# Attention in half-rows of TensorE: both heads' scores and both halves of a transposed block emitted in turn, middle rows as one full-row product

## Chip, core and metric

One core of one Trainium2 chip. The metric is device time in microseconds; the kernel before takes 741.76 us in the median of three runs.

## What is computed

Attention over 16 (batch, head) pairs with pooled queries, then two feed-forward blocks on its 1152 x 512 output:

```python
q_pool = q.reshape(B, H, S // 2, 2, D).mean(axis=3)       # B 2, H 8, S 1152, D 64
scores = scale * np.matmul(q_pool, k.transpose(0, 1, 3, 2))
scores = scores - np.max(scores, axis=-1, keepdims=True)
attn = np.exp(scores); attn = attn / (np.sum(attn, axis=-1, keepdims=True) + 1e-09)
x = np.matmul(attn, v)                                    # rows to 1152 tokens x 512
g = x @ w_gate; x = (g / (1 + np.exp(-g)) * (x @ w_val)) @ w_out      # d_ff 1536
h = x @ w_in; out = (np.maximum(h, 0) + alpha * np.minimum(h, 0)) @ w_out2   # d_ff 2048
```

## The kernel before

**Stages.** Heads are handled in eight pairs: head 0 of a pair lies on partitions 0 to 63, head 1 on 64 to 127. A pair has 576 pooled query rows per head, cut into nine units of 128 rows of scores: four units for each head, and one middle unit that holds the first 64 rows of both heads. After the eight pairs come the feed-forward blocks (contract, L791; out1, L851; out2, L880).

**A unit.** The scores of a unit stand against 1152 keys in three cuts of 448, 448 and 256 columns, each in one PSUM bank (four banks "s"). Queries and keys are split into a high and a low part in a rounded format ("fed"), and three products (high-high, low-high, high-low; TERMS) make one cut: L639, a matmul over one 64-row half of the array. The middle unit is not split: L633, plain fp32 from the raw q and k ("plain"), one 64 x 64 corner of the array for each head. DVE copies a cut out of PSUM with a running extreme (L643), ACT takes the exponential with a row sum (L645). Then the 128 x 1152 block is transposed on TensorE (L666): each of nine chunks as two transposes, rows 0 to 63 and rows 64 to 127, 64 columns out of each, collected five and four at a time in banks "t" (three of them). A bank is moved to SBUF by ACT (L679) or DVE (L673); a counter gives DVE a quarter of them. When a group of units is through (5/9, then 4/9 of a pair) the product with the values follows (L700): plain fp32, all 128 rows, 64 columns for each head, so the two heads run side by side; nine key chunks x two heads in a group. Row sums are inverted (L711 to L714), sent through DRAM and multiplied in by POOL.

**Order.** Nothing is emitted in loop order. Each operation is a task with an engine, a planned duration, a priority and buffers; Plan.run fills engine after engine in planned time and emits in that order. PE has three queues: PE (whole array) and PE0, PE1 (ROWS: the 64-row halves), the two halves planned independently, each task on its own planned end. On the chip all of them stand in one instruction stream. Going from half rows to whole rows has a planned price ("turnon"). While nothing fits early on, both halves idle, small matmuls on zeros (L361) are emitted. Weights of the feed-forward blocks are loaded from the first transpose of the last pair on ("begun") and split by ACT and DVE (L476 to L484).

## Time and profile before

| what | us |
|---|---|
| median of three runs (739.19 to 751.92) | 741.76 |
| profiled execution | 734.53 |
| its span, first to last instruction | 732.7 |
| PE busy, share of the span | 98% |
| DVE, ACT, POOL busy | 65%, 49%, 12% |
| mean granted TensorE clock | 0.959 |

The span is that of the profiled execution; the other 1.8 us lie around it. A matmul's duration in a row includes its passage through the array, and matmuls overlap: what a stream of them costs is read from the distance of starts. The granted clock is a share of 2.4 GHz; 0.50 is 1.2 GHz.

### The profile page before, as it was taken

How to read it: one execution, taken by the hardware profiler on the slowest of the kernel's cores; microseconds unless marked ns; L12 is line 12 of the kernel's file. 1: busy time of each engine (PE TensorE's matmuls, PEld its weight loads, DVE VectorE, ACT ScalarE, POOL GpSimd, SP SyncE). 2: the span in 40 equal slices, each digit the busy share in tenths (PEclk: the TensorE clock that was granted, in tenths of full speed). 3: DMA queues.
4: the chain of work that ended last, by engine and by line, in shares of the span. 5: the costliest groups of instructions: out<-in, count | busy, mean ns of one | idle time of the engine just before them, and what ended most of it. 6: DMA issues, size and time to landing. Idle time of an engine off the chain costs nothing.

```text
span 732.7 us, 12409 instructions
## 1 busy us (share of the span) xinstructions
PE 720.4 (98%) x4919; PEld 609.3 (83%) x4919; DVE 473.7 (65%) x976; ACT 355.4 (49%) x651; POOL 87.9 (12%) x83
## 2 busy tenths in 40 slices
PE   6999999999999999999999999999999999999998
PEld 4657676857676767899999999999999899898886
DVE  4455555757564657899987569557889729754332
ACT  3346566858574768545444343223067546342210
POOL 2222222333312101100000000002400000000000
PEclk7589979999997999999999999999999999999999
DMA  4213121311210202433435113310213401100002
GB/s 129 65 34 98 32 84 36 97 65 51 66 50 33 79 19 86 159 146 115 160 129 167 64 57 116 116 58 14 102 58 116 138 36 61 54 1 0 1 34 96
DMA packets 16650, 55.37 MB, mean 76 GB/s; under 512 B 2192, under 2 KB 2832, under 8 KB 16592
## 3 DMA queue, kind: packets, MB, share of 16 engines
q1 hardware_dynamic: 16512, 54.46, 21.9%
q8 instruction: 38, 0.62, 0.3%
q14 instruction: 20, 0.16, 0.1%
q10 hardware_dynamic: 80, 0.11, 0.1%
HBM read 52.17 MB, written 2.40 MB: 74 GB/s over the span
## 4 chain that ended last, share of the span: by engine, by line
PE 96%; DVE 1%; DMA 1%; ACT 1%; issue 0%; DVEq 0%
PE bank L791 33%; PE bank L880 14%; PE bank L639 12%; PE bank L700 10%; PE bank L851 10%; PE bank L666 10%; PE bank L633 6%; DMA plain<-in_kt 1%; PE bank L361 0%; DMA plain<-in_qt 0%; DVE magnitudes L480 0%; ACT weights L481 0%; PE bank L713 0%; ACT et L679 0%; DVE et L673 0%
## 5 line engine op out<-in xcount | busy, mean ns | idle before, releaser
L791 PE MATMUL bank<-xh,weights 128*128 128x384 f32 x960 | 253.6, 337 | 0.6 <-DVE weights L484 0.6
L791 PEld LDWEIGHTS bank<-xh,weights 128*128 128x128 f32 x960 | 174.4, 188 | 3.5 <-DVE weights L484 1.0
L791 PE MATMUL bank<-xl,weights 128*128 128x384 f32 x480 | 161.4, 336 | 0.0
L639 PE MATMUL bank<-fed 64*128 64x448 f32 (+1 forms) x576 | 130.0, 391 | 6.5 <-ACT fed L569 4.5
L666 PEld LDWEIGHTS bank<-ident,plain 64*128 64x128 f32 x1296 | 92.2, 145 | 39.3 <-issue 18.0
L643 DVE TENSOR_SCALAR_CACHE_REDUCE plain<-bank,stats 128x448 f32<-128x448 f32 (+1 forms) x144 | 82.5, 579 | 58.6 <-PE bank L639 42.7
L666 PE MATMUL bank<-ident,plain 64*128 64x64 f32 x1296 | 108.8, 238 | 0.8 <-DVE et L673 0.3
L679 ACT ACTIVATE et<-bank 128x320 f32<-128x320 f32 (+1 forms) x216 | 79.7, 423 | 56.8 <-PE bank L666 52.8
L639 PEld LDWEIGHTS bank<-fed 64*128 64x128 f32 x576 | 87.5, 206 | 16.7 <-issue 6.3
L645 ACT ACTIVATE plain<-plain,stats 128x1152 f32<-128x1152 f32 x72 | 90.8, 1267 | 11.5 <-DVE plain L643 10.7
L791 PEld LDWEIGHTS bank<-xl,weights 128*128 128x128 f32 x480 | 90.2, 188 | 1.2
L700 PE MATMUL bank<-et,plain 128*64 128x256 f32 (+1 forms) x576 | 79.9, 431 | 0.0
L880 PE MATMUL bank<-wr,fed 128*128 128x512 f32 (+1 forms) x279 | 70.4, 387 | 0.0
L700 PEld LDWEIGHTS bank<-et,plain 128*64 128x64 f32 x576 | 43.7, 145 | 30.4 <-issue 6.1
L643 DVE TENSOR_SCALAR_CACHE_REDUCE plain<-bank 128x448 f32<-128x448 f32 x72 | 44.7, 621 | 30.7 <-PE bank L639 29.2
L831 ACT ACTIVATE plain<-bank,signs 128x384 f32<-128x384 f32 x48 | 27.9, 582 | 70.3 <-PE bank L791 70.1
L880 PEld LDWEIGHTS bank<-wr,fed 128*128 128x128 f32 x279 | 51.1, 188 | 10.4
L832 DVE SCALAR_TENSOR_TENSOR plain<-bank,signs,plain 128x384 f32<-128x384 f32 x48 | 29.5, 615 | 36.2 <-ACT plain L831 36.2
L851 PE MATMUL bank<-fed,wr 128*128 128x384 f32 x264 | 52.2, 338 | 0.0
L673 DVE COPY et<-bank 128x256 f32<-128x256 f32 x72 | 30.4, 422 | 27.5 <-PE bank L666 21.7
L851 PEld LDWEIGHTS bank<-fed,wr 128*128 128x128 f32 x264 | 46.8, 188 | 0.0
L633 PE MATMUL bank<-plain 64*64 64x448 f32 (+1 forms) x96 | 44.9, 572 | 0.0
(75 smaller groups left out, 775.6 us busy)
## 6 DMA issues: line engine op xcount, KB each, us to landing
plain<-in_w_out SPq DMA_DIRECT2D x28, 512.0 KB
plain<-in_w_in SPq DMA_DIRECT2D x16, 512.0 KB
plain<-in_w_gate SPq DMA_DIRECT2D x12, 512.0 KB
plain<-in_w_val SPq DMA_DIRECT2D x12, 512.0 KB
plain<-in_vt SPq DMA_DIRECT2D x8, 576.0 KB
plain<-in_qt SPq DMA_DIRECT2D x7, 576.0 KB
plain<-in_kt SPq DMA_DIRECT2D x7, 576.0 KB
plain<-rowd SPq DMA_DIRECT2D x16, 144.0 KB
```

The source lines that it names most:

```text
L633: add(ROWS[h], 4 * w / 2400.0 + 0.0075, lambda s=s, rows=rows, js=js, w=w: nc.tensor.matmul(s.ap[rows, :w], x.qm.ap[rows], x.kn.ap[rows, j ...
L639: nc.tensor.matmul(s.ap[:, :w], x.qhl.ap[rows, a * SQ + c0:a * SQ + c0 + P], x.khl.ap[rows, b * S + js.start:b * S + js.stop], start=k == ...
L643: add(DVE, dve(w) + 0.056, lambda s=s, js=js, w=w, i=i: nc.vector.tensor_scalar(e.ap[:, js], s.ap[:, :w], 1.0, m(i - 1) if i else None, AL ...
L645: add(ACT, act(S, True, True), lambda: nc.scalar.activation(e.ap, e.ap, AF.Exp, bias=m(2), scale=-1.0, accum_out=x.sums.ap[:, n:n + 1]), p ...
L666: add(ROWS[h], HALFTURN, lambda t=t, c=c, ks=ks, rows=rows: nc.tensor.transpose(t.ap[:, c * D:c * D + D], e.ap[rows, ks:ks + P], ident[row ...
L673: go(dst, t.ap[:, :size * D].rearrange("p (c q) -> p c q", q=D))
L679: add(ACT, act(size * D), lambda move=move: move(lambda d, s: nc.scalar.activation(d, s, AF.Copy)), pr, [(t, 0)], [tok], [t, b])
L700: nc.tensor.matmul(acc.ap[rows, :n], x.vn.ap[:, h * SQ + kc * D:h * SQ + kc * D + D], ets[h][blk].ap[:, at:at + n], start=kc == 0, stop=kc ...
L791: nc.tensor.matmul(acc.ap[:, :TB], l[:, cs], r[:, c, ts], start=c == 0 and a == 0, stop=c == KC - 1 and a == 2)
L832: add(DVE, dve(TB) + 0.056, lambda: nc.vector.scalar_tensor_tensor(u.ap, a.ap[:, :TB], sign(), u.ap, ALU.mult, ALU.max), prio, [a], [u], [ ...
L851: nc.tensor.matmul(acc.ap[:, :TB], l[:, os_], r, start=n == 0 and m == 0, stop=n == len(g) - 1 and m == 2)
L880: nc.tensor.matmul(acc.ap[:, :width], l, r[:, cols], start=n == 0 and m == 0, stop=n == len(g) - 1 and m == 2)
```

## The change

The two half-row queues become one (HALF). A score task now emits the matmul of head 0 and of head 1 right after each other, so a unit is done for both heads at a time (five steps a pair: the middle one and four double ones). A transpose task holds a whole bank's worth, upper and lower half in turn. The middle unit becomes a whole-row product: the queries of both heads stand in two 64 x 64 corners of a 128 x 128 block whose rest is zero (corner), split into high and low like the others, three terms; POOL makes the corners with four copies of 64 x 64 per pair. Eviction of a transposed bank goes to whichever of ACT and DVE the planner finds (EITHER). The planner now prices a switch between half and whole rows in both directions; its priorities (KNOB) are others, among them vstep 0.321 for 0.007: the product with the values is planned key chunk by key chunk. The first pair's loads come in two pieces for both heads where there were pieces per head. The feed-forward code is not touched.

```diff
-ROWS = ("PE0", "PE1")
+HALF = "PEH"
+EITHER = "ACT or DVE"
...
+            full, half = self.pick(PE, now, hold[PE], port), self.pick(HALF, now, hold[PE], port)
+            if full and half:
+                if full[0] + (knobs["push"] if halves else -knobs["stay"]) <= half[0]:
+                    heapq.heappush(wait[HALF], half)
+                    half = None
                 else:
...
+            if full or half:
+                begin((full or half)[2], now, knobs["turnon"] if halves != bool(half) else 0.0)
...
+            elif now < 40.0 and not self.classes["acc"]["next"]:
+                self.idle()
...
+    corner = stat.tile([P, 2, 2 * P], F32R, name="corner")
+    nc.gpsimd.memset(corner.bitcast(F32), 0.0)
...
-        x.qcuts = [(0, 0, N0), (0, N0, SQ), (1, 0, SQ)] if first else [(None, 0, SQ)]
-        x.kcuts = [(0, *c) for c in CUTS] + [(1, 0, S)] if first else [(None, 0, S)]
+        x.qcuts = [(None, 0, N0), (None, N0, SQ)] if first else [(None, 0, SQ)]
+        x.kcuts = [(None, *c) for c in CUTS] if first else [(None, 0, S)]
...
-        add(POOL, gp(D), lambda: nc.gpsimd.tensor_scalar(x.qm.ap, x.qn.ap[:, :D], QSCALE, 1.0, ALU.mult, ALU.mult), K["first"] if first else s0, [(x.qn, i) for i, c in enumerate(x.qcuts) if c[1] == 0], [x.qm], [x.qn, x.qm])
+        for a in range(2):
+            for h in range(2):
+                r = rows(h)
+                add(POOL, gp(D), lambda a=a, h=h, r=r: nc.gpsimd.tensor_scalar(x.qm.ap[r, a * P + h * D:a * P + h * D + D], qpart(a, slice(0, D), r).bitcast(F32), 1.0, 1.0, ALU.mult, ALU.mult),
...
-    OF = [[0, 1, 5, 2, 6], [3, 7, 4, 8]]
-    OF0 = [[1, 2, 5, 0, 6], [3, 7, 4, 8]]
+    OF = [[0, 1, 2], [3, 4]]
+    OF0 = [[1, 0, 2], [3, 4]]
...
-            for h in range(2) if head == 2 else ():
-                rows = slice(h * D, h * D + D)
-                add(ROWS[h], 4 * w / 2400.0 + 0.0075, lambda s=s, rows=rows, js=js, w=w: nc.tensor.matmul(s.ap[rows, :w], x.qm.ap[rows], x.kn.ap[rows, js], start=True, stop=True),
...
-                add(ROWS[head], beside(w), go, pos + turn("qk", p, n), rd, [(s, head)], [s, x.qhl, x.khl])
...
+                    for k, (a, b) in enumerate(TERMS):
+                        nc.tensor.matmul(s.ap[:, :w], x.qm.ap[:, a * P:a * P + P], x.khl.ap[:, b * S + js.start:b * S + js.stop], start=k == 0, stop=k == 2)
+                add(PE, 3 * mm(w), go, at, [(x.qm, a, h) for a in range(2) for h in range(2)] + x.kread(js.start, js.stop), [(ss[0], 2)], [ss[0], x.qm, x.khl])
...
+                    for h in range(2):
+                        rows = slice(h * D, h * D + D)
+                        nc.tensor.matmul(ss[h].ap[:, :w], x.qhl.ap[rows, a * SQ + c0:a * SQ + c0 + P], x.khl.ap[rows, b * S + js.start:b * S + js.stop], start=k == 0, stop=k == 2)
+                add(HALF, beside(w), go, at, rd, [(s, 2) for s in ss], [*ss, x.qhl, x.khl])
...
-                    add(ROWS[h], HALFTURN, lambda t=t, c=c, ks=ks, rows=rows: nc.tensor.transpose(t.ap[:, c * D:c * D + D], e.ap[rows, ks:ks + P], ident[rows, rows]),
...
+                    for c in range(size):
+                        ks = (at + c) * P
+                        for h in range(2):
+                            rows = slice(h * D, h * D + D)
+                            nc.tensor.transpose(ts[h].ap[:, c * D:c * D + D], e.ap[rows, ks:ks + P], ident[rows, rows])
...
+                add(HALF, HALFTURN * size, go, pr + turn("t", p, n), [(e, 0)], [(t, 0) for t in ts] + mark, [*ts, e])
...
-                if moved[0] * K["evd"] % 36 >= K["evd"]:
...
+                    task = add(EITHER, 0.0, None, q, [(t, 0)], [tok], [t, b])
```

What it moves, by the order of instructions on PE. Half-way through a pair in the kernel before, the middle unit (L633, 64 x 64) and the transposes and scores around it:

```order
L639 MATMUL bank<-fed 128x256
L633 MATMUL bank<-plain 64x448
L639 MATMUL bank<-fed 128x256 x2
L666 MATMUL bank<-ident,plain 128x64 x4
L633 MATMUL bank<-plain 64x448
L666 MATMUL bank<-ident,plain 128x64 x5
L633 MATMUL bank<-plain 64x448
L666 MATMUL bank<-ident,plain 128x64 x5
L633 MATMUL bank<-plain 64x448
```

Six such products a pair stand apart, one head at a time, with runs of four to seven transposes between them. The same unit after the change (L649), with transposes (L687) and the product with the values (L722):

```order
L722 MATMUL bank<-et_98,plain 64x320
L722 MATMUL bank<-et_100,plain 64x320
L687 MATMUL bank<-ident,plain 128x64 x8
L649 MATMUL bank<-fed,corner 128x448 x6
L687 MATMUL bank<-ident,plain 128x64 x10
L649 MATMUL bank<-fed,corner 128x256 x3
L722 MATMUL bank<-et_98,plain 64x320
L722 MATMUL bank<-et_100,plain 64x320
```

Nine whole-row matmuls in two blocks take the place of the six. The second place is the product with the values. Before, its 18 matmuls of a group follow each other without a break, scores and transposes in uneven runs ahead of them:

```order
L639 MATMUL bank<-fed 128x448 x3
L639 MATMUL bank<-fed 128x256 x3
L639 MATMUL bank<-fed 128x448
L666 MATMUL bank<-ident,plain 128x64 x3
L639 MATMUL bank<-fed 128x448
L666 MATMUL bank<-ident,plain 128x64
L700 MATMUL bank<-et_93,plain 64x256
L700 MATMUL bank<-et_95,plain 64x256
L700 MATMUL bank<-et_93,plain 64x256
L700 MATMUL bank<-et_95,plain 64x256
L700 MATMUL bank<-et_93,plain 64x256
```

After, the transposes (L687) stand in tens and eights, the scores (L657) in even numbers, and the product with the values is spread over them:

```order
L687 MATMUL bank<-ident,plain 128x64 x8
L657 MATMUL bank<-fed 128x448 x8
L687 MATMUL bank<-ident,plain 128x64 x10
L657 MATMUL bank<-fed 128x448 x4
L722 MATMUL bank<-et_94,plain 64x256
L722 MATMUL bank<-et_96,plain 64x256
L687 MATMUL bank<-ident,plain 128x64 x8
L722 MATMUL bank<-et_94,plain 64x256
L722 MATMUL bank<-et_96,plain 64x256
L722 MATMUL bank<-et_94,plain 64x256
L722 MATMUL bank<-et_96,plain 64x256
L687 MATMUL bank<-ident,plain 128x64 x10
```

In all, the instruction stream of PE changes between half rows, whole rows and the 64 x 64 corner 137 times before and 216 times after, in a middle pair 26 times after. Of the 288 banks of transposed blocks DVE moves 72 before and 156 after. Until the first product with the values 118 matmuls on zeros stand behind the first score matmul; before, 33.

## Rows read from the trace of the kernel before

**Rows 1.** Page, busy time of the engine; the chain that ended last, by line.
```profile
PE 720.4 (98%) x4919; PEld 609.3 (83%) x4919; DVE 473.7 (65%) x976; ACT 355.4 (49%) x651; POOL 87.9 (12%) x83
...
PE bank L791 33%; PE bank L880 14%; PE bank L639 12%; PE bank L700 10%; PE bank L851 10%; PE bank L666 10%; PE bank L633 6%; DMA plain<-in_kt 1%; PE bank L361 0%; DMA plain<-in_qt 0%; DVE magnitudes L480 0%; ACT weights L481 0%; PE bank L713 0%; ACT et L679 0%; DVE et L673 0%
```
**Rows 2.** Windows of one pair and the feed-forward stage: busy PE, PEld, DVE, ACT, POOL.
```profile
148.29:180.59 32.30, 32.30 (x321) 22.36 (x323) 19.42 (x67) 21.87 (x49) 10.58 (x10) 1.00 0.20 66
301.31:732.70 431.39, 427.47 (x2317) 407.15 (x2316) 302.03 (x431) 170.52 (x256) 14.16 (x13) 1.00 0.23 82
```
**Rows 3.** Chain in order of time (start, us, what): products with the values.
```profile
44.74 6.95 PE bank L700 x36
...
148.29 5.00 PE bank L700 x36
...
180.59 5.00 PE bank L700 x36
...
283.05 2.84 PE bank L700 x20
```
**Rows 4.** Chain of one pair, 148.29 to 180.59, by line.
```profile
by line: PE bank L639 28.7%; PE bank L700 28.0%; PE bank L666 27.9%; PE bank L633 14.6%; PE bank L713 0.8%
```
**Rows 5.** Timeline of PE (start, us) in that pair: the middle unit.
```profile
154.30 0.96 PE L633 MATMUL bank<-plain 64*64 64x448 f32 x2
...
155.54 0.40 PE L666 MATMUL bank<-ident,plain 64*128 64x64 f32 x4
155.87 0.96 PE L633 MATMUL bank<-plain 64*64 64x448 f32 x2
```
**Rows 6.** Timeline of PE: transposes and scores in runs.
```profile
78.05 0.87 PE L639 MATMUL bank<-fed 64*128 64x448 f32 x6
...
161.81 0.97 PE L639 MATMUL bank<-fed 64*128 64x448 f32 x4
...
170.09 0.52 PE L666 MATMUL bank<-ident,plain 64*128 64x64 f32 x10
```
**Rows 7.** Chain in order of time: whole-row matmuls of 384 columns.
```profile
363.08 4.16 PE bank L791 x24
```
**Rows 8.** Timeline of PE in the last pair: product with the values, broken once.
```profile
282.98 2.91 PE L700 MATMUL bank<-et,plain 128*64 128x320 f32 x20
285.82 0.64 PE L666 MATMUL bank<-ident,plain 64*128 64x64 f32 x11
286.39 2.65 PE L700 MATMUL bank<-et,plain 128*64 128x320 f32 x16
288.97 0.77 PE L666 MATMUL bank<-ident,plain 64*128 64x64 f32 x14
290.02 1.61 PE L666 MATMUL bank<-ident,plain 64*128 64x64 f32 x18 [0.27 <-DVE et L673]
```
**Rows 9.** Page, groups: scores, transposes, DVE evictions (busy us, mean ns of one).
```profile
L639 PE MATMUL bank<-fed 64*128 64x448 f32 (+1 forms) x576 | 130.0, 391 | 6.5 <-ACT fed L569 4.5
...
L666 PE MATMUL bank<-ident,plain 64*128 64x64 f32 x1296 | 108.8, 238 | 0.8 <-DVE et L673 0.3
...
L673 DVE COPY et<-bank 128x256 f32<-128x256 f32 x72 | 30.4, 422 | 27.5 <-PE bank L666 21.7
```
**Rows 10.** Windows: start-up and two falls of the clock (third figure from the right).
```profile
10.00:35.00 25.00, 24.88 (x119) 16.90 (x120) 13.67 (x37) 10.12 (x19) 4.82 (x9) 0.50 0.18 61
...
90.00:100.00 10.00, 10.00 (x60) 6.45 (x60) 3.37 (x11) 5.09 (x12) 4.97 (x3) 0.51 0.39 119
220.00:226.00 6.00, 6.00 (x39) 2.78 (x38) 3.24 (x9) 2.26 (x4) 0.67 (x1) 1.00 0.28 98
226.00:236.00 10.00, 10.00 (x68) 8.18 (x69) 5.01 (x19) 6.46 (x14) 3.79 (x2) 0.51 0.00 0
```
**Rows 11.** Chain in order of time: start-up.
```profile
3.45 5.70 DMA plain<-in_kt
...
16.41 2.37 PE bank L361 x22
```

More of the change, by code (lines that the diff above doesn't have):

```diff
@@ L46 @@
 class Plan:
-    LAT = {PE: 0.21, ROWS[0]: 0.21, ROWS[1]: 0.21, ACT: 0.15, DVE: 0.13, POOL: 0.1, SP: 0.05}
+    LAT = {PE: 0.21, HALF: 0.21, EITHER: 0.15, ACT: 0.15, DVE: 0.13, POOL: 0.1, SP: 0.05}
     def __init__(self):
@@ L136, in fits @@
     def fits(self, t):
-        return all(b.slot is not None or self._spot(b) for b in t.bufs)
+        taken = {}
+        for b in t.bufs:
+            if b.slot is not None:
+                continue
+            c = self.classes[b.cls]
+            k = taken.get(b.cls, 0)
+            if c["next"] + k != b.n:
+                return False
+            if not k and not self._spot(b):
+                return False
+            if k and sum(s.buf is None and not (s.cells & self.held) for s in c["slots"]) <= k:
+                return False
+            taken[b.cls] = k + 1
+        return True
     def pick(self, e, now, ahead, port):
@@ L162, in run @@
         self.held = set()
-        free = {PE: self.first, ROWS[0]: self.first, ROWS[1]: self.first, ACT: 0.0, DVE: 0.0, POOL: 1.7, SP: 0.6}
-        self.wait = wait = {e: [] for e in free}
+        free = {PE: self.first, ACT: 0.0, DVE: 0.0, POOL: 1.7, SP: 0.6}
+        self.wait = wait = {e: [] for e in (*free, HALF, EITHER)}
         moved = 2.15
@@ L224, in run @@
                 item = self.pick(e, now, hold[e], port)
+                other = self.pick(EITHER, now, 0.0, port) if e in (ACT, DVE) else None
+                if other and (not item or other[0] + (knobs["lean"] if e == DVE else 0.0) < item[0]):
+                    if item:
+                        heapq.heappush(wait[e], item)
+                    item = other
+                    t = item[2]
+                    t.eng = e
+                    t.dur, t.emit = t.ways[e]
+                elif other:
+                    heapq.heappush(wait[EITHER], other)
@@ L530, in prep @@
         x.qread = lambda c0, c1, h=None: of(x.qcuts, x.qhl, c0, c1, h)
-        x.kraw = lambda h, c0, c1: [(x.kn, 0)] if not first else [(x.kn, 2)] if h else [(x.kn, int(c0 > 0))]
+        x.kraw = lambda c0, c1: [(x.kn, int(first and c0 > 0))]
         x.kread = lambda c0, c1, h=None: of(x.kcuts, x.khl, c0, c1, h)
@@ L620, in unit @@
     def unit(x, p, n, pos):
-        e, st = buf("e"), buf("st")
-        x.last = e
-        head, c0 = UNITS[n]
-        m = lambda i: st.ap[:, i:i + 1]
-        hs = range(2) if head == 2 else (head,)
-        for i in range(3):
-            s = buf("s")
+        kinds = ["mid"] if n == 0 else [0, 1]
+        es, sts = [buf("e") for _ in kinds], [buf("st") for _ in kinds]
+        c0 = D + (n - 1) * P
+        for i in range(NCUT):
+            ss = [buf("s") for _ in kinds]
             js = slice(*CUTS[i])
@@ L643, in unit @@
-            add(DVE, dve(w) + 0.056, lambda s=s, js=js, w=w, i=i: nc.vector.tensor_scalar(e.ap[:, js], s.ap[:, :w], 1.0, m(i - 1) if i else None, ALU.mult, ALU.min, accum_out=m(i)),
-                pos + turn("max", p, n), [(s, h) for h in hs] + [(st, i - 1)] * (i > 0), [(st, i), (e, i)], [s, e, st])
-        add(ACT, act(S, True, True), lambda: nc.scalar.activation(e.ap, e.ap, AF.Exp, bias=m(2), scale=-1.0, accum_out=x.sums.ap[:, n:n + 1]),
-            pos + turn("exp", p, n), [(st, 2)], [(e, i) for i in range(3)] + [(x.sums, n)], [e, st, x.sums], late=0.1)
```

157 lines of the change are left out of this document (68 added, 89 removed).

## Prediction

> **What bounds the kernel now.** I read the page first, then the chain in order of time, then one pair of heads in close-up. TensorE is busy 98% of the span and the chain runs through PE lines nearly throughout; DVE and ACT are at 65% and 49% [rows 1]. So only what PE does can move the end by much. The run has three parts. The feed-forward stage, from 301.31 us on, is 431.4 us of PE work [rows 2] and its code is not touched. The first product with the values stands at 44.74 us and the same product of the last pair at 283.05 [rows 3]: 238.3 us for seven pairs, 34.0 each. A pair at the full clock takes 32.3 us (148.29 to 180.59) [rows 3]. In that pair the chain goes 28.7% through scores, 27.9% through transposes, 28.0% through the product with the values, 14.6% through the middle unit [rows 4]: 9.3, 9.0, 9.0 and 4.7 us. DVE and ACT are busy 19.4 and 21.9 of the 32.3 us [rows 2], so PE is the limit inside the pair too.
>
> **The change, part by part, for one pair at the full clock.**
>
> Transposes. Nine chunks x nine units are 81 upper and 81 lower halves. Where ten stand behind a product and both halves are at hand, they take 0.52 us [rows 6], of which the last one's own passage is 0.24 [rows 9]: the starts of five pairs lie within 0.28 us, 0.06 to 0.07 a pair. Four in a single half take 0.40 [rows 5], that is three steps in 0.16, about the same. So two halves side by side cost what one costs, and today's 9.0 us for 81 pairs, 0.11 each, says that mostly one half runs alone: each half waits for its own bank. Emitted in turn: 81 x 0.062 = **5.0 us**, 4.0 less.
>
> Scores. Four matmuls in one half take 0.97 us [rows 6], less 0.39 of passage [rows 9] three steps of 0.19 to 0.20. Six spread over both halves take 0.87 [rows 6]: 0.48 for the starts, where one half alone would need up to 1.0 for five steps. In turn, 24 pairs of 448 columns at 0.20 and 12 of 256 at 0.118 (0.20 scaled with the columns, an estimate) are **6.2 us** for 9.3.
>
> Middle unit. One product of 448 columns is two rows and takes 0.96 us. Started at 154.30 it is over at 155.26; four transposes follow at 155.54, the next product at 155.87 [rows 5]. While the 64 x 64 shape runs, nothing else does, not even the other head's product. After, nine whole-row matmuls: 24 of 384 columns take 4.16 us [rows 7], 0.173 each, so 0.202 for 448 and 0.116 for 256, together **1.6 us** for 4.7. The four corner copies go to POOL, busy 10.6 of 32.3 us with ten instructions [rows 2], a pair ahead of their use; hidden by its idle time. Without that cover they would cost at most four times its mean of 1.06, 4.2 us once, ahead of a middle unit.
>
> Product with the values. The same 36 rows, **9.0 us**, but cut into some 13 blocks where two stood. A cut has a price: from 282.98 to 288.97 the product and eleven transposes take 5.99 us, the unbroken product 5.00 [rows 3, 8], six steps of transposes 0.37; 0.62 us is left for going out and back. The lower bound is what the edges of a block show by themselves: ten pairs of rows take 2.84 us from 282.98 on, eighteen take 5.00, so eight take 2.16, 0.27 each, and 0.14 of the 2.84 is edge. I take 0.35 a trip, about the middle, for 10.5 more trips: **3.7 us**; the ends are 1.5 and 6.5. Row-sum inverse, 0.8% [rows 4]: **0.3**.
>
> Sum: 5.0 + 6.2 + 1.6 + 9.0 + 3.7 + 0.3 = 25.8 us for 32.3.
>
> What then comes late. DVE takes over 84 more evictions, 10.5 a pair at 0.42 us [rows 9]: 19.4 + 4.4 = 23.8 us, 92% of 25.8; ACT falls to 21.9 - 4.4 = 17.5. PE will have to wait now and then. The place is the bank: a transpose task needs two of the three banks "t", so the second eviction of the task before must be through. Such a wait shows once today, 0.27 us behind a DVE eviction [rows 8]. Bounds: none, or 0.27 before each of a pair's 18 tasks, 4.8 us. I take 1.4 (about five tasks), since the order puts scores or a product between nearly all tasks: **27.2 us a pair**.
>
> [...]
>
> Clock. In two stretches of 10 us the granted clock is 0.51, that is 1.2 of 2.4 GHz, and PE gets through 60 and 68 rows [rows 10]. The second comes right behind a middle unit (154.30 in [rows 5] and two periods of 32.3 us are 218.9), in whose stretch of 6 us 39 rows start, where the pair's mean is ten per us [rows 2]; the first lies at the same place of its pair. They make up the difference of 34.0 and 32.3, 12 us in seven pairs. With the 64 x 64 products gone I take these falls as gone (the bound: they stay, +12).
>
> Steady part: 7 x 27.2 = 190.4 for 238.3, **-47.9 us**.
>
> Start-up. The first keys land at 9.15 us; then come 25 us at half clock, with 22 fillers on zeros in one piece [rows 10, 11]. The first key piece now holds both heads, so the first score comes perhaps 1 us later. Up to the first product with the values PE then has 21 + 9 pairs of scores, 45 of transposes, the middle unit and 118 fillers: at twice the times above 8.4 + 2.1 + 5.6 + 3.2 us, and 12.6 for fillers if each takes the 0.107 that 22 in 2.37 us show [rows 11], 32 us behind 10.5. If the clock rises at once it is half. I take 36 to 37 us for 44.7, **-8**; bounds 0 and -15.
>
> Tail. From 283.05 to 301.31, 18.3 us, DVE and ACT also split the first weights; that work stays. **-2**, bounds +3 and -4. Feed-forward: **0**.
>
> Sum: 732.7 - 47.9 - 8 - 2 = 674.8 us span, 676.6 with the 1.8 us around it. That is 0.921 of the profiled execution's 734.5. The median is 7.2 us above that execution, so on its scale 741.76 x 0.921 = **683 us**.
>
> **Rivals.**
>
> 1. *Evictions set the pace.* If each transpose task waits its 0.27 us, a pair takes 30.6 us: 3.4 x 7 = 24 more, 707 us. For it: DVE at 92%, three banks where a task takes two. Against: ACT at 68% and the choice of either engine. It is a gain still.
>
> 2. *The halves do not run in pairs.* If neighbours in the stream start one after another, 81 pairs of transposes cost 0.124 each, 10.0 us for 5.0: 5 x 8 = 40 us of the gain go, 723. Against: ten in 0.52 us [rows 6]. For: no long stretch of today's trace shows more than ten matmuls per us [rows 2], so a high pace over several microseconds is not shown. [...]
>
> 3. *Slower: the clock.* PE waits of 0.3 us before many tasks could bring it to 1.2 GHz for long. Each us of span at that level does half a us of work [rows 10]. Today at least 45 us lie at the lower level. The gain of 58 us is used up when 116 us more do, and 2% is lost at 146: 757 us and up. For it: start-up stays low for 25 us with PE busy 24.9 of 25 [rows 10]. Against: through the pair of [rows 2] PE worked without a break and the clock stayed full, and the change puts more work into each us.
>
> **How the numbers follow.** My forecast 0.66, rival 1 0.20, rival 2 0.07, rival 3 0.07, in over half of it slower by more than 2%. Low end: no stalls (-10) and the best start-up (-7), or trips at their lower price (-15), 667. High end: rival 1, 708. Within my own case it is 667 to 696. About 2% (15 us) is what a measurement of this kernel tells from no change. Faster by over 2% (under 727): 0.66 + 0.20 + most of rival 2, 0.91. Within 2%: 0.05. Slower: 0.04.
>
> **What the next profile would show.** Pairs of heads (distance of the inverse L735) at 27 us; the middle unit L649 at 0.2 us a matmul with nothing of 64*64 left; runs of ten transposes in about 0.5 us; DVE near 90% in the steady part; no fall of the clock between 50 and 230 us; the feed-forward stage at 431 us. I am wrong if PE shows long idle times before L687 (rival 1), if ten transposes take 0.8 us or more (rival 2), or if the clock stands at 0.5 in several stretches (rival 3).

## The result and the profile after

The changed kernel takes 663.24 us (median of four runs, 663.13 to 663.53); the kernel before, run beside it, took 740.48 (four runs, 733.58 to 751.92). The ratio is 0.8986, with a 95% interval of 0.8922 to 0.9049. The forecast was 683, with a range of 667 to 708: right in direction and for the steady part, but the time lies below the low end, because the start-up gained 20.4 us where 8 were forecast. The profiled execution has a span of 661.3 us, beside 732.7 before.

The page of the kernel after (busy time of the engines; the chain that ended last, by line) answers to [rows 1]. L657 is the scores, L687 the transposes, L722 the product with the values, L649 the middle unit.

```profile
PE 654.9 (99%) x4994; PEld 555.7 (84%) x4994; DVE 498.4 (75%) x1058; ACT 326.7 (49%) x565; POOL 93.1 (14%) x107
...
PE bank L813 38%; PE bank L902 15%; PE bank L722 12%; PE bank L873 11%; PE bank L657 9%; PE bank L687 8%; PE bank L649 2%; PE bank L374 1%; PE bank L371 1%; ACT plain L667 0%; DVE allsums L733 0%; PE bank L735 0%; ACT L836 0%; DVE et L697 0%; ACT plain L726 0%
```

PE is still the limit: of the 71.4 us by which the span is shorter, PE's busy time gives 65.5 (720.4 to 654.9 us). Its attention lines have shrunk, and no line of another engine has more than 0% of the chain, although DVE is up from 65 to 75%.

Windows of the kernel after: the start-up; first product with the values to that of the last pair; from there to the first feed-forward product; the feed-forward stage; and one pair in mid-run. They answer to [rows 2, 10]. Columns: busy PE, PEld, DVE, ACT, POOL, each with its count, then the granted clock, DMA share, GB/s.

```profile
5.30:24.30 19.00, 19.00 (x298) 16.75 (x295) 17.02 (x55) 12.36 (x26) 9.69 (x14) 1.00 0.50 172
24.32:214.18 189.86, 188.88 (x2222) 122.78 (x2218) 166.83 (x547) 132.50 (x265) 62.08 (x68) 1.00 0.23 77
214.18:226.60 12.42, 11.89 (x131) 6.35 (x131) 11.07 (x24) 8.50 (x18) 6.38 (x4) 1.00 0.24 87
226.61:661.30 434.69, 431.00 (x2338) 408.18 (x2336) 302.63 (x433) 171.52 (x256) 13.46 (x13) 1.00 0.23 82
...
106.34:133.07 26.73, 26.73 (x317) 17.53 (x316) 22.99 (x78) 18.84 (x39) 10.31 (x12) 1.00 0.24 79
```

The pair takes 26.73 us where [rows 2] showed 32.30, with nearly the same number of matmuls (317 and 321): PE gets through 11.9 of them per us instead of 9.9. DVE is busy 86% of it. The trace's records of the granted clock have 1.00 from 5.2 us to 660.6, where [rows 10] had 0.50 for 25 us in one go.

The chain of that pair, by line and its first steps in order of time, answers to [rows 3, 4].

```profile
by line: PE bank L722 38.9%; PE bank L657 28.2%; PE bank L687 25.0%; PE bank L649 7.4%; PE bank L735 1.0%
...
106.41 2.30 PE bank L722 x16
108.71 0.46 PE bank L687 x10
109.17 0.78 PE bank L657 x8
109.95 0.25 PE bank L687 x6
```

PE lines alone fill the pair, without one step of DVE or ACT: in this pair no eviction is late. The product with the values comes in pieces of 4 to 16 where blocks of 36 stood.

The timeline of PE in the same pair (start, us) answers to [rows 5, 6].

```profile
111.16 0.52 PE L687 MATMUL bank<-ident,plain 64*128 64x64 f32 x10
111.61 0.76 PE L722 MATMUL bank<-et,plain 128*64 128x320 f32 x4
112.30 0.46 PE L687 MATMUL bank<-ident,plain 64*128 64x64 f32 x8
112.69 1.49 PE L649 MATMUL bank<-fed,corner 128*128 128x448 f32 x6
114.10 0.53 PE L687 MATMUL bank<-ident,plain 64*128 64x64 f32 x10
114.56 0.62 PE L649 MATMUL bank<-fed,corner 128*128 128x256 f32 x3
```

Ten transposes take 0.52 us in task after task, not only once: of the 68 such runs in the kernel, 67 take 0.53 us or less. The middle unit is 2.1 us of whole-row products (1.49 and 0.62), and transposes stand right against them; [rows 4] had 4.7.

### The profile page after: what moved, and what is told of

Read it like the earlier page. It is cut to its first block, busy times and chain, and to the rows that moved or that the text cites. A ratio compares the mean times of both kernels' runs of the same rounds, so it can differ in the third digit from the quotient of the medians.

```text
span 661.3 us, 12547 instructions
## 1 busy us (share of the span) xinstructions
PE 654.9 (99%) x4994; PEld 555.7 (84%) x4994; DVE 498.4 (75%) x1058; ACT 326.7 (49%) x565; POOL 93.1 (14%) x107
## 4 chain that ended last, share of the span: by engine, by line
PE 98%; DVE 1%; ACT 1%; issue 0%; ACTq 0%; DVEq 0%
PE bank L813 38%; PE bank L902 15%; PE bank L722 12%; PE bank L873 11%; PE bank L657 9%; PE bank L687 8%; PE bank L649 2%; PE bank L374 1%; PE bank L371 1%; ACT plain L667 0%; DVE allsums L733 0%; PE bank L735 0%; ACT L836 0%; DVE et L697 0%; ACT plain L726 0%
## 5 line engine op out<-in xcount | busy, mean ns | idle before, releaser
L722 PE MATMUL bank<-et,plain 128*64 128x256 f32 (+1 forms) x576 | 89.9, 422 | 0.2 <-ACT plain L726 0.2
L687 PEld LDWEIGHTS bank<-ident,plain 64*128 64x128 f32 x1296 | 54.5, 138 | 41.7 <-ACT et L702 18.7
L663 DVE TENSOR_SCALAR_CACHE_REDUCE plain<-bank,stats 128x448 f32<-128x448 f32 (+1 forms) x144 | 79.2, 578 | 6.9 <-PE bank L657 4.0
L697 DVE COPY et<-bank 128x256 f32<-128x256 f32 (+1 forms) x156 | 66.5, 450 | 17.7 <-PE bank L687 16.5
L657 PE MATMUL bank<-fed 64*128 64x448 f32 (+1 forms) x576 | 78.9, 366 | 0.0
L702 ACT ACTIVATE et<-bank 128x320 f32<-128x320 f32 (+1 forms) x132 | 51.4, 410 | 44.2 <-PE bank L687 40.7
L687 PE MATMUL bank<-ident,plain 64*128 64x64 f32 x1296 | 70.5, 230 | 0.6 <-ACT et L702 0.5
L902 PEld LDWEIGHTS bank<-wr,fed 128*128 128x128 f32 x279 | 51.1, 188 | 10.4
L854 DVE SCALAR_TENSOR_TENSOR plain<-bank,signs,plain 128x384 f32<-128x384 f32 x48 | 29.5, 614 | 35.3 <-ACT plain L853 35.3
L722 PEld LDWEIGHTS bank<-et,plain 128*64 128x64 f32 x576 | 33.2, 135 | 24.6 <-issue 8.2
L657 PEld LDWEIGHTS bank<-fed 64*128 64x128 f32 x576 | 49.7, 188 | 4.0 <-issue 2.4
L492 ACT ACTIVATE magnitudes<-plain 128x1024 f32<-128x1024 f32 x34 | 38.8, 1142 | 15.6 <-DMA plain<-in_w_in 4.4
```

What stands on the lines that cost most here:

```text
L492: add(ACT, act(2 * DM, True), lambda: nc.scalar.activation(mag.ap, word(1, F32), AF.Abs), prio, reads=got, writes=[mag], bufs=[raw, mag])
L657: nc.tensor.matmul(ss[h].ap[:, :w], x.qhl.ap[rows, a * SQ + c0:a * SQ + c0 + P], x.khl.ap[rows, b * S + js.start:b * S + js.stop], start=k ...
L663: add(DVE, dve(w) + 0.056, lambda s=s, js=js, w=w, i=i, m=m, e=e: nc.vector.tensor_scalar(e.ap[:, js], s.ap[:, :w], 1.0, m(i - 1) if i els ...
L687: nc.tensor.transpose(ts[h].ap[:, c * D:c * D + D], e.ap[rows, ks:ks + P], ident[rows, rows])
L697: go(dst, t.ap[:, :size * D].rearrange("p (c q) -> p c q", q=D))
L702: task.ways = {ACT: (act(size * D), lambda move=move: move(lambda d, s: nc.scalar.activation(d, s, AF.Copy))), DVE: (dve(size * D), lambda ...
```

## Experiments

The kernel after repeats within 0.4 us. The kernel before does not: its runs lie between 730 and 752 us, with mean granted clocks between 0.934 and 0.984 where they were recorded. So variants are set against 663.2, or read by stretches of their profiles. An edit that changes durations or tasks also makes the plan order all other tasks anew; it is said where that is so. "First V" is the first product with the values.

Two questions came out of the result. Start-up had shrunk from 44.7 to 24.3 us, far more than forecast; and the steady part was right, but is it right for the reasons given?

### Start-up: is it the late keys and PE's gap, or the kind of work?

Four experiments. The 1.2 GHz of what stands above and of the expectations is the granted clock of 0.50: there 22 fillers of 128 columns start 0.107 us apart (from 16.21 us on, kernel before), 1.2 columns a ns; at 1.00 fourteen start 0.056 us apart (from 8.07 us on, kernel after). The 2.4 GHz is an estimate, twice those 1.2; the 0.056 us are 2.3 columns a ns. **b_key**: the kernel before, with the load of alpha moved back, so that ACT's key load no longer waits.

```
-    add(SP, 0.65, lambda: nc.sync.dma_start(alpha_sb, alpha), -5.0, ...)
+    add(SP, 0.65, lambda: nc.sync.dma_start(alpha_sb, alpha), 3.0, ...)
```

> The kernel before with one load moved: the small load of alpha goes behind the value loads on SP, so that ACT's load of the first keys is the eighth transfer and not the ninth and no longer waits for the first query piece to land. All other engines keep their order. Theory S (start-up): PE has nothing from 5.0 to 9.8 us, the clock falls in that gap and stays at 1.2 GHz long after; with keys some 1.5 to 3 us earlier the first score starts at 7 to 8 us and, if the clock holds, the first product with the values comes 10 us or more earlier: 720 to 728 us where before has 733 to 742. Rival A (the kind of work): the slow start comes from single-half scores and 64 x 64 products, the gap does not matter; only the 2 us of the earlier keys are won: 731 to 740.

**b_fill**: the kernel before, with 90 more fillers on zeros that bridge PE's gap ahead of the first score.

```
     for i in range(K["warm"]): idle(512)
+    for i in range(90): idle_rows(P)
```

> The kernel before with 90 more small matmuls on zeros right behind the eight warm-up ones, which fill PE's gap up to about 9.8 us; keys land as late as before. Theory S: the clock stays at 2.4 GHz through the gap and well into the start-up, the first product with the values moves from 44.7 to 30 to 36 us and the kernel takes 720 to 730 us. Rival A: the first score still starts near 9.8 us and the clock falls as soon as single-half scores run alone; first product with the values at 42 us or later, 732 to 742 us.

**a_late**: the changed kernel, with ACT's first key load behind the landing of the first query piece, which gives PE the gap of the kernel before.

```
-            load(lambda: x.kn.ap[r, c], kt[p, r, c], pr, x.kn, (x.kn, tok), eng=eng)
+            load(lambda: x.kn.ap[r, c], kt[p, r, c], pr, x.kn, (x.kn, tok), eng=eng, head=(lambda: nc.scalar.activation(warm, x.qn.ap[:, :1], AF.Copy)) if eng == ACT else None)
```

> The changed kernel with the key load of ACT put behind the landing of the first query piece (an activation on ACT reads it first), as it stood before; PE's order is unchanged. Theory S: the first score moves from 6.1 to 9 to 10 us, PE has a gap of 3 to 4 us, the clock falls to 1.2 GHz and stays there for more than 10 us; the first product with the values at 34 to 42 us for 24.3, the kernel at 674 to 682 us. Rival A: only the 3 to 4 us of the later keys: 666 to 668 us, clock at 1.0 throughout.

**a_nofill**: the changed kernel without its 142 fillers on zeros.

```
-    plan.idle = lambda: idle_rows(P)
+    plan.idle = lambda: None
```

> The changed kernel without the 142 small matmuls on zeros, all else in the same order. If they keep the clock up (part of theory S): the clock is at 1.2 GHz for 10 us or more of the start-up and the kernel takes 670 to 680 us. If the paired work does it alone: clock falls only briefly or not at all, 660 to 666 us.

Measured, one run each: b_key 742.85, b_fill 741.78, beside 733.86 for the kernel before on that chip; a_late 670.72; a_nofill 662.55. The first two lie within the spread of the kernel before, so their times tell nothing; b_key's is outside both of its ranges, and a_late's is between its two. The profiles tell more. The windows, one fence for each kernel: b_key,

```profile
8.60:42.70 34.10, 34.10 (x199) 24.53 (x199) 20.12 (x56) 16.46 (x32) 11.47 (x12) 0.50 0.23 77
```

b_fill, up to the fall of the clock and after it,

```profile
4.40:14.30 9.90, 9.37 (x121) 8.47 (x121) 5.88 (x13) 3.14 (x6) 2.95 (x5) 1.00 0.64 190
14.30:48.40 34.10, 34.10 (x200) 23.64 (x201) 19.07 (x52) 16.16 (x32) 7.79 (x7) 0.50 0.16 53
```

and a_late: the gap, the stretch at the lower level, and what follows.

```profile
6.60:11.90 5.30, 0.03 (x1) 0.00 (x0) 0.00 (x0) 0.59 (x2) 1.19 (x5) 0.73 0.51 197
9.00:15.80 6.80, 3.86 (x25) 2.99 (x26) 3.24 (x9) 1.77 (x4) 0.00 (x0) 0.50 0.05 21
15.90:31.80 15.90, 15.90 (x254) 14.12 (x252) 13.36 (x46) 10.43 (x21) 7.74 (x7) 1.00 0.37 114
```

The gap theory falls for the kernel before. b_key starts its first score at 5.44 instead of 9.80 and b_fill has PE busy 9.37 of 9.90 us at the higher level; both then spend 34.1 us in one go at a granted clock of 0.50, with PE busy all the time, and reach first V at 40.5 and 44.1. In that stretch of b_key the halves run mostly one at a time: 15 of its 90 transposes start within 20 ns of the row before them (in strict pairs it would be 45), where the kernel after has 34 of 90 up to first V. In the changed kernel the gap does cost the clock, but only for 6.8 us: it rises again at 15.9, before the first middle unit at 17.97, with scores of both heads and fillers (which all use the upper half). Of a_late's 7.5 us, 5.8 are the later first score. Fillers are not the reason why the clock stays up: a_nofill has no fall after the clock's rise at 9.6 us, although PE has idle time there.

```profile
9.60:23.70 14.10, 11.94 (x144) 8.61 (x142) 13.34 (x46) 10.76 (x22) 6.39 (x7) 1.00 0.39 128
```


### One part alone: the corner product in the kernel before

**b_corner** puts the whole-row middle unit, with its four corner copies, into the kernel before; the plan then orders the other tasks anew, and the evictions stay divided as they were. **b_ck** adds the earlier key load of b_key.

```
-                add(ROWS[h], ..., nc.tensor.matmul(s.ap[rows, :w], x.qm.ap[rows], x.kn.ap[rows, js], ...))
+                    for k, (a, b) in enumerate(TERMS):
+                        nc.tensor.matmul(s.ap[:, :w], x.qm.ap[:, a * P:a * P + P], x.khl.ap[:, b * S + js.start:b * S + js.stop], ...)
```

> The kernel before with one part of the change alone: the middle unit as three whole-row products of a corner tile, in place of two 64x64 products; scores, transposes and blocks of V stay as they were. Theory A (the lower clock comes with the kind of work, and the 64x64 products, in which PE starts few rows, are what sets it off): 3.1 us less a pair (4.7 to 1.6) and no falls of the clock between 50 and 230 us; 8 x 3 = 24 us and some 12 to 20 us of clock, so 690 to 708 us, start-up still long (first V at 35 to 44). Rival A2 (single-half scores and transposes are enough to set it off): 24 us less at most, falls of the clock stay in mid-run and in the start-up, 712 to 722. Rival (the middle unit was beside other work after all): no more than 5 us less, 730 or more.

> The kernel before with the whole-row middle unit (as b_corner, 700.7) and in addition the first key load 4 us earlier (as b_key), scores and transposes still half by half. It splits the start-up of 44.7 against 24.3 us: b_corner has its first V at 36.9, with its first score at 9.55 and the clock first at its higher level at 26.7. Theory W (work in one half at a time keeps the clock at its lower level until the whole-row products come, whenever it starts): first V at 32 to 34, the clock rises only with the middle unit, about 697 us. Rival G (the gap of 3.6 us in which PE has nothing keeps the clock low): the clock is at the higher level before 12 us, first V at 26 to 29, 690 to 693 us.

Measured: b_corner 700.66 us (700.3 to 704.78), ratio 0.9442, interval 0.938 to 0.9504; b_ck 698.75 (696.49 to 700.53). Windows of b_corner: from the first score, behind the clock's rise, one pair.

```profile
9.55:26.70 17.15, 17.15 (x101) 14.81 (x101) 10.72 (x27) 6.77 (x12) 5.88 (x10) 1.00 0.30 99
26.70:36.90 10.20, 10.20 (x124) 8.88 (x123) 8.66 (x31) 8.74 (x21) 4.36 (x6) 1.00 0.29 80
126.30:155.78 29.48, 28.70 (x317) 22.48 (x316) 19.89 (x67) 21.37 (x49) 10.65 (x12) 1.00 0.24 72
```

Windows of b_ck: the stretch at the lower level and what follows.

```profile
8.70:22.40 13.70, 12.97 (x76) 11.24 (x76) 9.05 (x22) 5.64 (x11) 8.42 (x10) 0.50 0.42 151
22.40:31.90 9.50, 9.43 (x116) 8.45 (x115) 7.79 (x27) 8.11 (x20) 2.61 (x6) 1.00 0.36 127
```

The 1.00 in b_corner's first row is not a measured clock: this trace's first record of the clock is at 26.7 us, and the view prints 1.00 ahead of it. The durations tell it. The first nine scores, all in one half, from the timelines of PE of b_corner and b_ck:

```profile
9.55 3.49 PE L649 MATMUL bank<-fed 64*128 64x448 f32 x9 [3.60 <-ACT fed L572]
```

```profile
5.51 1.82 PE L649 MATMUL bank<-fed 64*128 64x448 f32 x9
```

3.49 against 1.82 us: b_corner ran at the lower level up to 26.7 us. In both kernels the clock rises while the whole-row products run (24.3 to 27.6 in b_corner, 19.0 to 22.7 in b_ck), and single-half work stands before them.

In mid-run the kernel with the corner saves about what the corner was priced at: 29.5 us a pair for 32.3, 2.8 less (forecast 3.1), and between 26.7 and 255 us the clock does not fall. It is not the product's time alone, though. Without the 64 x 64 products between them the blocks are longer: b_corner's stream changes shape some 60 times, where the kernel before had 137. And DVE has come into the chain of that pair (L653 copies scores, L721 is the row sums, L683 evicts; more on the row sums under the evictions):

```profile
by line: PE bank L710 30.6%; PE bank L649 29.0%; PE bank L676 21.4%; DVE plain L653 7.8%; DVE allsums L721 4.7%; PE bank L642 2.8%; DVE et L683 2.6%; issue 0.9%; PE bank L723 0.9%; DVE allinv L722 0.1%; DVEq L653 0.1%
```

The start-up stays long. So theory A holds for b_corner in its time and in mid-run. In the start-up theory W fits b_ck best (first V at 31.95), without being exact: the clock stood at its higher level from 5.3 to 8.7 us too, under scores of one half. No 64 x 64 product is left in b_ck, and the clock still stood at 0.50 for 13.7 us; in mid-run it fell once more, for 3.4 us at 46.3. b_corner in turn held 1.00 behind its rise with the halves mostly apart (10 of 72 transposes up to first V start within 20 ns of the row before). So work in one half at a time goes with the lower level in the start-up, but does not bring it about everywhere.

### One part undone: 64 x 64 products in the changed kernel

**a_oldmid** puts the old middle unit back, both heads' products next to each other; the plan orders the other tasks anew.

```
-                    for k, (a, b) in enumerate(TERMS):
-                        nc.tensor.matmul(s.ap[:, :w], x.qm.ap[:, a * P:a * P + P], ...)
+                    for h in range(2):
+                        rows = slice(h * D, h * D + D)
+                        nc.tensor.matmul(s.ap[rows, :w], x.qm.ap[rows], x.kn.ap[rows, js], start=True, stop=True)
```

> The changed kernel with the middle unit put back to 64x64 products in float32, both heads' products next to each other. Theory A (64x64 products set the lower clock off): about 25 us for the products themselves, if a head's two products still run one after the other and nothing beside them, or 12 if the two heads' products run beside each other; on top of it falls of the clock to 0.5 in mid-run, so 690 to 715 us. Rival A2 (the single-half scores and transposes of the kernel before set it off): the clock stays at 1.0, 675 to 688 us. If the products' neighbours hide them: 664 to 668.

Measured: 670.66 us (669.58 to 671.6), 7.4 over the kernel after, between two of the ranges. The timeline of PE, one pair's middle unit:

```profile
116.88 1.72 PE L643 MATMUL bank<-plain 64*64 64x448 f32 x8
118.99 0.65 PE L643 MATMUL bank<-plain 64*64 64x256 f32 x4
```

Eight rows are four products, since one is two rows: 0.43 us each, where one alone took 0.96 in [rows 5]. The twelve rows take 2.4 us, the nine of the corner product 2.1. So the shape is not what cost so much; running one head at a time was. This corrects a reading of the prediction, that beside a 64 x 64 product not even the other head's runs: emitted next to each other, they do. Seven pairs take 193.0 us against 189.9. The rest is at the ends: first V at 27.07 behind a wait of PE of 1.6 us, and a fall of the clock for 3.4 us at 24.4 and at 232.6. Between these it does not fall, 64 x 64 or not.

### Turn by turn: are the halves paired by the order, or by themselves?

Three edits that leave all tasks in their order, on every engine, and only change the order inside a task. **a_thalf**: the upper halves of a transpose task first, then the lower ones.

```
-                    for c in range(size):
-                        for h in range(2):
+                    for h in range(2):
+                        for c in range(size):
```

> The changed kernel with one edit: inside a transpose task the four or five upper halves are emitted first and the lower ones behind them, where they alternated; all else stands in the same order. Theory T1 (strict turn is what pairs the halves; behind another half's instruction nothing overtakes): a run of ten transposes goes from 0.52 us to 0.8 to 0.9, a pair costs 5 us more, 36 to 42 us in all, 700 to 706. Theory T2 (the two row halves run independently, a short look ahead suffices, so what matters is that both halves' work is at hand in one task): 0 to 5 us more, 663 to 668.

**a_qhalf**: per cut, head 0's three products, then head 1's (first pair of heads as it was).

```
-                    for h in range(2):
+                    for h, j in ([(0, k), (1, k)] if x.p == 0 else [divmod(2 * k + i, 3) for i in range(2)]):
+                        rows, (a, b) = slice(h * D, h * D + D), TERMS[j]
```

> The changed kernel with one edit: of each cut of scores head 0's three products are emitted first and head 1's three behind them, where they alternated (the first pair of heads is left as it is); all else stands in the same order. Theory T1 (strict turn is needed): up to 36 pairs of products a pair of heads at 0.39 in place of 0.20, 6 us a pair, 7 x 6 = 42, 700 to 706 us. Theory T2 (halves run independently with some look ahead): three products of 0.2 us wait for the other half only at the edges, 0.2 to 0.4 us for each of some 12 cuts, 0 to 5 us a pair if cuts stand alone, so 663 to 690, near the low end where cuts follow each other.

**a_both**: both, and in the first pair of heads too.

> The changed kernel with strict turn taken out everywhere: in each transpose task the upper halves first, in each cut of scores head 0's three products first, and this in the first pair of heads too; both heads' work stays in one task and in the same order of tasks. Theory D (work for both halves within a task's reach is enough, turn itself is worth 6.0 us in the transposes and 8.2 in the scores, and it is not what keeps the clock): the two losses add, 663.2 + 14.2 = 677 us, clock at its higher level from below 11 us on without a fall, first V at 25 to 28. Theory C (in the start-up strict turn is what keeps the clock up): the clock falls in the first 25 us as in the kernel before, first V at 30 to 38, 684 to 692 us. If the two losses hide behind each other: 670 to 673.

Measured: a_thalf 669.38 (669.37 to 671.77), a_qhalf 671.58 (670.37 to 672.83), a_both 680.6 (680.34 to 680.67). Timeline of PE of a_thalf:

```profile
128.71 0.64 PE L687 MATMUL bank<-ident,plain 64*128 64x64 f32 x10
...
131.47 0.47 PE L687 MATMUL bank<-ident,plain 64*128 64x64 f32 x8
```

Windows of a_both: the start-up and one pair.

```profile
6.10:25.00 18.90, 18.82 (x290) 17.06 (x288) 16.52 (x54) 11.77 (x24) 9.29 (x14) 1.00 0.46 158
113.50:142.80 29.30, 29.30 (x317) 20.13 (x316) 23.41 (x77) 18.88 (x40) 10.30 (x12) 1.00 0.23 73
```

Four upper halves and then four lower ones take 0.47 us, as in turn (0.46); five and five take 0.64 for 0.52. The halves overlap by themselves to a degree, and turn buys the rest: 6 us in the transposes, 8 in the scores, 17 in both together, 3 more than the sum, which none of a_both's ranges had. T1, some 40 us for either, is refuted.

In mid-run strict turn is worth 2.6 us a pair (29.3 against 26.7). That a_both's 29.3 is near b_corner's 29.5, where the two heads are planned apart, is no proof that turn is all that the new order adds: a_both has the many changes of shape of the kernel after, and PE alone in its chain from 110 to 170 us, where b_corner has few changes and 15% of DVE.

```profile
by line: PE bank L722 36.3%; PE bank L657 30.5%; PE bank L687 25.8%; PE bank L649 6.6%; PE bank L735 0.9%
```

The start-up is another matter: a_both has no fall of the clock after its rise at 6.1 us, and its first V stands at 25.0, 0.7 behind the kernel after. So strict turn is not what keeps the clock up there. What is left is that both heads' work lies within reach; no run gives the kernel before that alone.

### The evictions: how much slack does the steady part have?

**a_quarter** gives every fourth eviction to DVE and the others to ACT; **a_vblock** and **a_v20** set the number that spreads the product with the values (vstep=0.321) to 0.007 and to 0.2. All three make the plan order DVE's, ACT's and POOL's work anew.

```
-                    task = add(EITHER, ...)
+                    moved[0] += 1
+                    if moved[0] % 4: add(ACT, ...)
+                    else: add(DVE, ...)
```

> The changed kernel with the evictions of turned blocks divided by a fixed rule, every fourth on DVE and the others on ACT, where the plan chose the engine (DVE takes most today). It moves some 5 us of work a pair from DVE (23 of 26.7 us busy) to ACT (18.8 of 26.7). Theory P (PE is the limit, evictions are in time on either engine): 661 to 668 us. Rival E (the evictions nearly set the pace, and ACT is late where it also has the exponentials): PE waits of 0.3 us and more in front of transposes, 2 us a pair and over, 678 to 700.

> The changed kernel with one number of the plan changed, so that the product with the values stands in few blocks again instead of being spread through the pair (85 instead of 216 changes between half-row, column-half and whole-row products up to the end of attention; other work moves a little with it). Theory P (a trip costs 0.35 us, as the prediction priced it, and PE alone sets the pace): some 60 trips less, 21 us less, 640 to 648 us. Rival E (the blocks of V were spread to give the evictions time; in one block of 9 us no transposes run, and then they come faster than three banks and DVE and ACT can empty them): PE waits for evictions behind DVE or ACT give back the gain or more, 660 to 685.

> The changed kernel with the blocks of the product with the values spread a little less: 173 changes of shape instead of 216 (a_vblock had 85 and took 689.7 us, with waits of PE for DVE's evictions and maxima). If trips cost 0.17 us a change and evictions still come in time, 43 changes less give back 7 us: 655 to 660, faster than the changed kernel. If the evictions already have no slack at the spread as it is, waits for DVE grow with the length of the blocks: the loss of a_vblock in proportion (a third of 26 us), 668 to 674.

Measured: a_quarter 679.95 (679.77 to 681.7), a_vblock 689.69 (684.59 to 691.61), a_v20 692.44 (690.3 to 693.09). a_vblock and a_v20 lie above all their ranges in the median. The chain of a_vblock between two long blocks of V:

```profile
123.98 0.57 PE bank L687 x10
124.55 0.02 issue
124.57 0.49 DVE et L697
125.06 0.49 DVE plain L663
125.56 0.04 issue
125.60 0.76 DVE et L697 x2
126.35 0.55 DVE plain L663 x2
```

Waits of PE of a_quarter between 83 and 199 us (in total, times, longest us):

```profile
PE bank L657 <- DVE plain L663: 2.6, 4, 0.7
PE bank L688 <- DVE et L698: 2.5, 4, 0.6
```

The chain of a_quarter from 110 to 170 us, by line (L735 is the row sums; the POOL lines split the next pair's queries and keys and scale and split the outputs), with its longest piece:

```profile
by line: PE bank L724 21.2%; PE bank L657 20.2%; PE bank L688 16.6%; DVE allsums L735 8.5%; POOL plain L754 4.7%; POOL xl L759 4.7%; PE bank L649 4.5%; POOL fed L587 3.8%; issue 2.6%; DVE fed L578 2.6%; POOL fed L577 2.3%; POOL xh L757 2.2%
...
145.31 2.55 DVE allsums L735
```

Fewer trips did not pay here. With V in a block of 36 rows, transposes and scores crowd between the blocks, and DVE, which must empty both their banks, comes into the chain; a pair takes 29.4 us. a_quarter's time is in the range of the second theory, and its pairs take 29.0 us, but the reason is another: PE waits for evictions 2.5 us in four pairs, where that theory asked for 2 us a pair, and the chain's lines above have no eviction. What they have is the row sums, one small operation on DVE (128 x 9). In four pairs running of a_quarter it takes 2.6 us, where the kernel after has 0.42, and that is 2.2 of the 2.3 us by which its pair is longer (11.6 of its 17 us lie in the seven pairs). It starts while POOL splits keys (L591) and ends with it, at 118.81 and 118.78 us in the pair that begins at 112.2; with POOL idle the same operation takes 0.17. So the new order put the row sums beside POOL's work, and the evictions behind them came late. a_v20 met neither of its expectations: a third of the way costs as much as the whole way or more, 31.3 us for the pair that begins at 115.3. Its row sums take 2.0 us; the rest of its loss stays open. Since all three move the plan's whole order, they price neither a trip nor the slack of the evictions by itself. No variant beats the changed kernel by more than a_nofill's 0.7 us in its one run.

## Why the prediction was off, step by step

The kernels side by side, in us, from the trace of each profiled execution:

| | first score | first V | seven pairs | then, to the end | span |
|---|---|---|---|---|---|
| before | 9.80 | 44.67 | 238.3 | 449.7 | 732.7 |
| b_corner | 9.55 | 36.91 | 208.6 | 453.1 | 698.6 |
| b_ck | 5.51 | 31.95 | 210.4 | 452.3 | 694.7 |
| a_both | 6.67 | 25.01 | 206.3 | 447.5 | 678.8 |
| after | 6.13 | 24.32 | 189.9 | 447.1 | 661.3 |

- **Steady part**: right, its total in part by luck. Forecast 190.4 us, measured 189.9. The mid-run pair has 26.73 us where the sum without stalls said 25.8. The stalls (1.4) are not there; PE's own work is 0.9 longer instead. Taking the forecast's other terms as they were, 22.1, the trips would come to 4.6 instead of 3.7; that is a remainder, since the chain books the edges of a trip under the other lines (scores 7.5 us for 6.2, transposes 6.7 for 5.0, product with the values 10.4 for 9.0). No run prices a trip by itself. (256 columns at the price of 448 scaled are 0.114 us, not 0.118; that is 0.05 us a pair.)
- **Clock in mid-run**: right that the falls would go; the reason was half of it. In b_corner taking out the 64 x 64 products was enough, though b_ck and a_v20, without them too, have a fall of 3.4 us each (at 46.3 and 188.6); a_oldmid shows that they may stay if both heads' products stand side by side. The two falls that the prediction named are 20.5 us at a granted clock of 0.50, 10 of its 12 us if half the work is lost there (an estimate); the rest lies at the first product with the values, up to 48.7 us.
- **Start-up**: the step that failed. Forecast -8 with bounds of 0 and -15, measured -20.4. The prediction put the first score at 10.5 us and first V some 26 us behind it, between the 32 us that it worked out for the lower level and half of them. Measured are 6.13 us and 18.2. So two things were missed. First, I let the start-up run largely at the lower level as before ("if the clock rises at once it is half"): 8.0 us. The clock rose at 5.2 us and stayed, where it had stood at the lower level for 27.3 us (7.7 to 35.0). Second, I put the first score 1 us later, because its key piece is twice as big; it came 3.7 us earlier (below): 4.4 us against the 10.5. Together they are the 12.4 us by which the term was too small. b_ck gives the same account from the other side: its first V at 31.95 less half of its 13.7 us at the lower level (an estimate) is 25.1, where a_both stands. Why the clock stays up is shown by exclusion only: neither the gap (b_fill) nor the keys (b_key), the fillers (a_nofill), strict turn (a_both) or the missing 64 x 64 products (b_ck) account for it. What exactly does stays open.
- **Tail and feed-forward**: right as a sum, by luck. Forecast -2 and 0; the tail lost 5.9 us and the stage behind it gained 3.3, since twenty rows of V now stand between the first feed-forward blocks. Together -2.6. Of the 5.9, up to 1.7 are a fall of the clock that the kernel before had there (294.4 to 297.8 us) and the kernel after has not.
- **The scale**: 683 came from multiplying the kernel before's higher median by the ratio of spans. That carried a spread of some 20 us over to a kernel that repeats within 0.4 us, at a mean clock of 0.999 or 1.0 in all four runs. The spread of the kernel before goes with its recorded clock only loosely (730.4 us at a mean of 0.984 and 749.5 at 0.934, but 735.0 at 0.960 and 750.1 at 0.961). Left unscaled the forecast is 676.6, 6.4 us nearer.

Together: 12.4 of the start-up, 6.4 of scale, 0.6 of the tail and 0.5 of the pairs are the 20 us between 683 and 663.2.

- **Rival 1** (evictions set the pace) did not happen: no waits of PE in the mid-run pair. a_vblock comes nearest to it, at 26 us, with evictions and copies of scores on DVE in its chain; a_quarter, at 17 us, is not this rival: its row sums are late. **Rival 2** (no pairing) is refuted by the 67 of 68 runs of ten transposes at 0.53 us or less. Nine steps in some 0.29 us (0.52 less a mean row of 0.23) are 32 ns each, 0.064 us a pair where this rival put 0.124. **Rival 3** (the clock) did not happen: the clock stayed up, and the start-up gained by it.

Where the first score gained: the chain of the kernel before at its start, its timeline, and the timeline of the kernel after: ACT's first key load and the first operation on what it brings.

```profile
0.71 2.71 DMA plain<-in_qt
```

```profile
3.45 0.54 ACTq L447 DMA_DIRECT2D plain<-in_kt  x1
...
9.17 1.35 ACT L569 ACTIVATE fed<-plain 64x448 fp32r<-64x448 f32 x3 [4.72 <-DMA plain<-in_kt]
```

```profile
1.37 0.41 ACTq L463 DMA_DIRECT2D plain<-in_kt  x1
...
5.37 1.50 ACT L585 ACTIVATE fed<-plain 128x448 fp32r<-128x448 f32 x3
```

In the program of the kernel before this load is the ninth DMA. It uses the semaphore of the first, a query load, again and waits for it; that one lands at 3.42 us. (The trace has the landings of all DMAs on eight semaphores, the query load's at 3.42 and the keys' at 9.15 us on the same one.) Two loads fewer stand ahead of it after, so it is the seventh and waits for nothing. The issue moves from 3.45 to 1.37 us. b_key, with the wait taken away, has its first score 4.4 us earlier; a_late, where the load is held behind the same query load by hand, 5.8 us later.

## What to carry to other kernels

Work for the two row halves of TensorE should lie side by side in its stream, in one task and in turn: in mid-run the turn is worth 2.6 us of 29.3 a pair. At the start, both heads' work within a task's reach went with the higher clock even without turn (a_both: 1.00 from 6.1 us to first V at 25.0). When a change removes loads, go through the order of all DMAs for semaphores that are used again; a load may start earlier or later though its own line did not move (here 2.08 us earlier). If a kernel spreads by more than the term in question and the change may end what spreads it, forecast from the profiled execution and do not scale to the median.

## What was not expected of the hardware

- The granted clock stood at 0.50 for 34.1 us in which PE was busy throughout, with scores and transposes mostly of one half at a time, 64 x 64 products, fillers and the first rows of V (b_key, b_fill). It held 1.00 in a_nofill, where PE had both heads' work and was idle for 2.2 of 14.1 us. What in the work decides was not told apart further.
- In a_thalf the two row halves start work out of the written order: the first score behind a task of ten transposes starts at 111.50 us, the last two of the ten at 111.52. With four uppers emitted first, eight take 0.47 us, 0.24 for the starts; four uppers and then four lowers at the three steps in 0.16 us of [rows 5] would need 0.32 for the starts alone (an estimate).
- In the kernels before and after, DVE's row sums (128 x 9) take 0.16 to 0.17 us in the six cases with POOL idle and 0.42 to 2.15 us in the ten beside an operation of POOL; all ten end 0.02 to 0.04 us behind it (the longest at 297.9 us before and at 60.8 after). The chain of a_quarter has 2.55.
- A view's clock of 1.00 ahead of the trace's first record of it is no reading; b_corner's nine scores there took 3.49 us for 1.82.
